# Weight columns in float32, an earlier cast of one batch, and eight output stores issued by ScalarE, in an attention and ReGLU kernel

## The chip, the cores and the metric

One core of one Trainium2 chip. The time is the device time of one execution in microseconds (us), and the median of several executions is quoted. All executions of the comparison before against after were in the fast state; slow ones elsewhere are named and left out.

## The reference

Causal attention for 8 batches of 8 heads (576 queries, 64 wide) over 16 "beacon" keys and values, which every query sees, and the batch's own 576; then a gated feed-forward layer over all 4608 rows (512 to 1536 to 512). Inputs and output are float32.

```python
k_all = np.concatenate([beacon_k, k], axis=2); v_all = np.concatenate([beacon_v, v], axis=2)
scores = scale * np.matmul(q, k_all.transpose(0, 1, 3, 2))
scores = np.where(causal, -1e9, scores)            # beacons never masked
a = np.exp(scores - scores.max(-1, keepdims=True)); a /= a.sum(-1, keepdims=True) + 1e-09
x = np.matmul(a, v_all)                            # then heads side by side: (4608, 512)
out = (np.maximum(x @ w_gate, 0.0) * (x @ w_val)) @ w_out
```

## The kernel before

It is one long, hand-ordered program. A list of steps says in which step a batch's attention and which groups of the feed-forward layer (FFN) run; the two are woven together so that TensorE always has matmuls. Loads, casts and transposes of a later batch are hung on these steps:

```python
def fetch(b, s0, late=1, held=False):
    at(s0, lambda: batches.update({b: Batch(b)}))
    for j, u in enumerate(LOADS):                  # k0 q1 k1 q2 k2 q3 k3 q0 k4 q4, then v0..v4
        s = s0 + j // 3
        at(s, lambda u=u, h=held and j == 0: batches[b].load(*u, h))      # SyncE
        at(s + late, lambda u=u: batches[b].cast(*u, pool))               # GpSimd
        if u[0] != "v":
            at(s + late + 1, lambda u=u: batches[b].turn(*u))             # SyncE, DMA transpose
fetch(2, s2 + 1, 3, True)
for b in range(3, B):
    fetch(b, BASE[b] - (7 if b == 3 else 5), 2 if b == 3 else 1)
```

GpSimd also runs the causal masks (`affine_select`) on what ScalarE's exponentials wrote. The end of the FFN, with its store:

```python
ob = pools["osb"].tile([P, d_model], FP32, name="ob")
nc.scalar.copy(ob[:, n], o[:, n])
m = self.m0 + ms * P
later_sp.append(                                   # issued at the next step
    lambda m=m, n=n, ob=ob: nc.sync.dma_start(out[m:m + P, n], ob[:, n]))
```

Every DMA signals a semaphore. SyncE and ScalarE take theirs in turn from one set of eight, GpSimd from another set; in the built program each DMA waits for the previous DMA on its own semaphore before it is issued (in the trace of before, SyncE's DMAs are on 101 and 103 to 109, GpSimd's on 111 to 118). A DMA raises its semaphore 16 times; it has landed when the last of the 16 has come.

## Time and profile before

| | before |
|---|---|
| time, median of 3 (range) | 391.03 us (390.40 to 392.42) |
| TensorE busy, of the profiled 391.3 us | 373.4 us (95%) |
| ScalarE busy | 190.6 us (49%) |
| waits of TensorE priced in the prediction | 4.10 us (stall B, 92 us), 1.7 us (stall A, 24 us) |

In a timeline each line gives start, duration, engine, source line, operation, output and inputs, how many of the same kind in a row, and in brackets how long the engine had been idle and what ended that. In the list of waits the three numbers are the total, the count and the longest. The change adds lines, so a source line of before has another number after: 391 becomes 403 (scores), 399 becomes 411 (exponential), 407 becomes 419 (mask), 454 becomes 466 (times v), 505, 508 and 514 become 517, 520 and 526 (FFN up, with its relu), 524, 527 and 530 become 536, 539 and 541 (FFN down, its copy, its store). Experiments built on one kernel have that kernel's numbers.

### The profile page before, as it was taken

Reading aid. Unit: us, or ns where it says so; the run is one execution under the profiler, and the core shown is the slowest. Engines: PE = TensorE matmul, PEld = TensorE weight load, DVE = VectorE, ACT = ScalarE, POOL = GpSimd, SP = SyncE. Lnnn points to the kernel's source line nnn. Section 1 sums busy time; section 2 is a strip of 40 time slices with the busy share of each in tenths; the row PEclk is TensorE's granted clock in tenths of the full one; section 3 lists DMA queues with packets and bytes.
Section 4 is the critical chain, followed back from the end, with each engine's and each line's share of the span. In section 5 each row is a group of like instructions: output and inputs, shape, how many; then the busy total and the mean of one; then the engine's idle time right before and its main releaser. Section 6 shows DMA issues by size and latency. Waiting matters only on the chain.

```text
span 391.3 us, 10203 instructions
## 1 busy us (share of the span) xinstructions
PE 373.4 (95%) x4297; PEld 189.9 (49%) x4297; DVE 199.2 (51%) x309; ACT 190.6 (49%) x271; POOL 123.0 (31%) x218
## 2 busy tenths in 40 slices
PE   7889999995999999999999999999999999999995
PEld 3454445542455555555555555555545544444443
DVE  4767577441374566346733674257525665412320
ACT  4763484336456553565447534655455523323321
POOL 1695464514443432252324242324320200000000
PEclk9989999998799999999999999999999999999999
DMA  7999999988896977697568855895310011002002
GB/s 214 194 206 186 171 186 218 167 190 185 157 170 138 207 141 164 139 217 131 108 156 179 158 110 126 193 138 128 86 55 2 2 55 54 2 28 80 3 27 87
DMA packets 148132, 50.44 MB, mean 129 GB/s; under 512 B 133616, under 2 KB 143600, under 8 KB 148080
## 3 DMA queue, kind: packets, MB, share of 16 engines
q1 hardware_dynamic: 139024, 44.48, 53.6%
q0 software_dynamic: 9056, 5.24, 9.8%
q8 instruction: 35, 0.57, 0.6%
q14 instruction: 17, 0.14, 0.2%
HBM read 38.34 MB, written 9.44 MB: 122 GB/s over the span
## 4 chain that ended last, share of the span: by engine, by line
PE 83%; DMA 7%; DVE 4%; SPq 2%; issue 1%; ACT 1%; POOL 1%; DVEq 0%
PE p L524 21%; PE p L505 20%; PE p L514 19%; PE p L454 8%; DMA wo<-in_moe_w_out_dram 4%; PE f L505 3%; PE p L391 3%; PE f L524 2%; DVE hT L516 2%; PE s L514 2%; DMA wide<-in_k_dram 1%; PE s L391 1%; PE ab L454 1%; DVE r L467 1%; SPq L275 1%
## 5 line engine op out<-in xcount | busy, mean ns | idle before, releaser
L516 DVE TENSOR_TENSOR hT<-g,p 128x512 bf16<-128x512 f32 x89 | 60.8, 684 | 107.2 <-PE p L514 76.5
L407 POOL TENSOR_SCALAR_AFFINE_SELECT e<-e 128x512 bf16<-128x512 bf16 (+2 forms) x80 | 46.3, 599 | 151.7 <-ACT e L399 151.5
L505 PE MATMUL p<-xT,wg 128*128 128x512 bf16 x356 | 93.2, 385 | 0.1
L514 PE MATMUL p<-xT,wv 128*128 128x512 bf16 x356 | 92.2, 382 | 0.0
L508 ACT ACTIVATE g<-p 128x512 f32<-128x512 f32 x89 | 52.8, 602 | 74.9 <-PE p L505 74.9
L524 PE MATMUL p<-wo,hT 128*128 128x512 bf16 (+1 forms) x396 | 85.5, 373 | 0.0
L399 ACT ACTIVATE e<-p 128x1024 bf16<-128x1024 f32 (+2 forms) x84 | 75.2, 966 | 14.8 <-PE p L391 14.8
L514 PEld LDWEIGHTS <-wv 128*128 128x128 bf16 x432 | 42.5, 99 | 53.4 <-issue 3.9
L467 DVE RECIPROCAL r<-p 128x256 f32<-128x256 f32 (+1 forms) x24 | 47.0, 1958 | 37.1 <-PE p L454 37.1
L524 PEld LDWEIGHTS <-hT 128*128 128x128 bf16 x444 | 42.1, 98 | 48.3 <-issue 0.8
L505 PEld LDWEIGHTS <-wg 128*128 128x128 bf16 x432 | 40.8, 99 | 49.3 <-issue 3.7
L527 ACT COPY ob<-p 128x512 f32<-128x512 f32 (+1 forms) x33 | 18.9, 573 | 66.3 <-PE p L524 66.3
L270 POOL CAST half<-raw 128x512 bf16<-128x512 f32 (+2 forms) x60 | 35.6, 619 | 14.5 <-DMA raw<-in_k_dram 9.7
L454 PEld LDWEIGHTS <-v 128*32 128x32 bf16 (+1 forms) x1408 | 27.8, 97 | 10.5 <-issue 5.3
L391 PEld LDWEIGHTS <-kT 64*128 64x128 bf16 x704 | 20.7, 97 | 25.1 <-issue 22.5
L454 PE MATMUL p<-e,v 128*32 128x80 bf16 (+4 forms) x1056 | 29.4, 231 | 1.6 <-DVE hT L516 1.0
L265 POOL CAST v<-raw 128x512 bf16<-128x512 f32 (+1 forms) x38 | 23.6, 644 | 13.3 <-DMA raw<-in_v_dram 13.3
L399 ACT ACTIVATE e<-s 128x1024 bf16<-128x1024 f32 (+2 forms) x28 | 25.6, 967 | 4.3 <-PE s L391 4.1
L391 PE MATMUL p<-qT,kT 64*128 64x80 bf16 (+3 forms) x528 | 23.0, 229 | 4.5 <-DMA qT<-half 4.1
L454 PE MATMUL p<-e,ones 128*32 128x80 bf16 (+4 forms) x528 | 24.3, 230 | 0.0
L505 PE MATMUL f<-xT,wg 128*128 128x512 bf16 x76 | 20.4, 393 | 0.3 <-DVE hT L516 0.3
L508 ACT ACTIVATE g<-f 128x512 f32<-128x512 f32 x19 | 11.4, 601 | 18.4 <-PE f L505 17.3
(81 smaller groups left out, 235.8 us busy)
## 6 DMA issues: line engine op xcount, KB each, us to landing
out_dram<-ob SPq DMA_DIRECT2D x35, 256.0 KB, 2.4
raw<-in_q_dram SPq DMA_DIRECT2D x25, 256.0 KB, 4.4
raw<-in_v_dram SPq DMA_DIRECT2D x24, 256.0 KB, 4.1
raw<-in_k_dram SPq DMA_DIRECT2D x19, 256.0 KB, 4.5
raw<-in_v_dram SPq DMA_DIRECT2D x8, 224.0 KB, 3.6
wo<-in_moe_w_out_dram POOLq DMA_DIRECT2D x2, 768.0 KB, 11.7
raw<-in_k_dram SPq DMA_DIRECT2D x6, 224.0 KB, 3.4
raw<-in_v_dram SPq DMA_DIRECT2D x8, 160.0 KB, 4.3
```

The costliest lines, as they stand in the source:

```text
L265: copy(self.v[:n, t].rearrange("p (h a d) -> p h a d", a=2, d=C), raw[:n].rearrange("p (h d a) -> p h a d", a=2, d=C))
L270: copy(h[:n], raw[:n])
L391: nc.tensor.matmul(self.s[:, a, c + j * n:c + (j + 1) * n], kT[rows, 2 * g + j, k0:k0 + P], qT[rows, 2 * g + j, q0:q0 + n], start=True, st ...
L399: nc.scalar.activation(e[:, :k * 4 * n].rearrange("p (k a x) -> p a k x", k=k, a=2), self.s[:, :, :k * 2 * n].rearrange("p a (k x) -> p a ...
L407: nc.gpsimd.affine_select(out=cols[:, :, :m], in_=cols[:, :, :m], pattern=[[0, 4], [1, m]], compare_op=ALU.is_ge, fill=0.0, base=base, cha ...
L454: nc.tensor.matmul(o[:, q0 - cq0:q0 - cq0 + n], w, e[:kr, 2 * (hh % 2) + hh // 2], start=(x == 0 and i == 0 and part != 1), stop=stop, ski ...
L467: nc.vector.reciprocal(self.r[:, :self.n], self.os[:, :self.n])
L505: nc.tensor.matmul(g[:, :n], wg[:, ki, nf * P:(nf + 1) * P], x[:, ki], start=(ki == 0), stop=(ki == KM - 1))
L508: nc.scalar.activation(gs[:, :n], g[:, :n], AF.Relu)
L514: nc.tensor.matmul(u[:, :n], wv[:, ki, nf * P:(nf + 1) * P], x[:, ki], start=(ki == 0), stop=(ki == KM - 1))
L516: nc.vector.tensor_mul(self.h[:, nf, c0:c1], gs[:, :n], u[:, :n])
L524: nc.tensor.matmul(o[:, n], self.h[:, nf, ms * P:(ms + 1) * P], wo[:, nf, n], start=(nf == 0), stop=(nf == NF - 1))
```

## The change

The intent is to relieve SyncE, whose one line of loads, transposes and stores is late for batch 2, and to let the weights' casting loads start behind the first loads. It has three parts: **W**, weights; **C**, the earlier cast of batch 2; **S**, the stores.

```diff
 # W: columns 256..384 of both matrices in float32 by SyncE, cast later; casting loads moved back
+        more_g, more_v = (load_w_more(x, 256, 384) for x in (moe_w_gate, moe_w_val))
-        after(3, lambda: load_w(wg, moe_w_gate, 256, 768))
-        after(3, lambda: load_w(wv, moe_w_val, 256, 768, (0,)))
-        after(4, lambda: first.cast("v", 4, pool))
-        mid[5] = lambda: load_w(wv, moe_w_val, 256, 768, (1,))
-        mid[6] = lambda: cast_w(wg, raw_g, 256, 1, pool)
+        after(3, lambda: first.cast("v", 4, pool))
+        after(3, lambda: load_w(wg, moe_w_gate, 384, 768))
+        after(4, lambda: load_w(wv, moe_w_val, 384, 768, (0,)))
+        mid[5] = lambda: load_w(wv, moe_w_val, 384, 768, (1,))
+        mid[6] = lambda: [cast_w(wg, raw_g, 256, 1, pool),
+                          cast_more(wg, more_g, 256, 384, pool)]
+        after(6, lambda: cast_more(wv, more_v, 256, 384, act))
 # C: batch 2's casts a step sooner, and a step's casts and loads all behind its FFN groups
-        fetch(2, s2 + 1, 3, True)
+        fetch(2, s2 + 1, 2, True)
-            for act_ in acts[:len(acts) // 2]:
+            early = len(acts) // 2 if s > BASE[2] else 0
+            for act_ in acts[:early]:
                 act_()
-            acts = acts[len(acts) // 2:]
+            acts = acts[early:]
 # S: the first two tiles' eight stores, issued by ScalarE right behind its copy
-                later_sp.append(
-                    lambda m=m, n=n, ob=ob: nc.sync.dma_start(out[m:m + P, n], ob[:, n]))
+                store = lambda e, m=m, n=n, ob=ob: e.dma_start(out[m:m + P, n], ob[:, n])
+                if self.m0 < 2 * M_TILE:
+                    store(nc.scalar)
+                else:
+                    later_sp.append(lambda store=store: store(nc.sync))
 # cut: load_w_more and cast_more themselves
```

More of the change, by code (lines that the diff above doesn't have):

```diff
@@ L363, in load_w_raw, with load_w_more, cast_more @@
         return raws
+    def load_w_more(src, n0, n1):
+        raw = stage.tile([P, d_model], FP32, name="raw")
+        for g in range(2):
+            nc.sync.dma_start(raw[:, 256 * g:256 * (g + 1)].rearrange("p (a n) -> p a n", a=2),
+                              src[2 * g * P:2 * (g + 1) * P, n0:n1].rearrange(
+                                  "(p a) n -> p a n", a=2))
+        return raw
+    def cast_more(dst, raw, n0, n1, cast):
+        cast(dst[:, :, n0:n1], raw.rearrange("p (k n) -> p k n", k=KM))
     def cast_w(dst, raws, n, g, cast):
```

## The prediction

> **What bounds the kernel now.** I read the page first: busy shares, then the slices.
>
> ```profile
> PE 373.4 (95%) x4297; PEld 189.9 (49%) x4297; DVE 199.2 (51%) x309; ACT 190.6 (49%) x271; POOL 123.0 (31%) x218
> PEclk9989999998799999999999999999999999999999
> ```
>
> TensorE is busy 95% of 391.3 us, nothing else above 51%: the end is set by TensorE's stream of matmuls, and only what leaves TensorE idle, or slow, can be won. It is idle for 391.3 - 373.4 = 17.9 us in all, and the granted clock dips twice, in slice 3 (19.6 to 29.3 us) and in slices 10 and 11 (88 to 108 us). Next, the list of waits for the whole run gives the idle places by cause (columns: us in total, times, longest):
>
> ```profile
> PE p L391 <- DMA qT<-half: 4.1, 1, 4.1
> PE ab L454 <- issue: 1.7, 1, 1.7
> PE f L524 <- DMA wo<-in_moe_w_out_dram: 0.5, 1, 0.5
> ```
>
> The rest is the start and shreds below 0.45 us. The first, **stall B**, is in TensorE's timeline (start, us, group; four matmuls of 512 columns are one group):
>
> ```profile
> 91.78 0.60 PE L391 MATMUL p<-qT,kT 64*128 64x128 bf16 x12
> 96.48 0.58 PE L391 MATMUL p<-qT,kT 64*128 64x80 bf16 x12 [4.10 <-DMA qT<-half]
> 97.00 1.89 PE L505 MATMUL p<-xT,wg 128*128 128x512 bf16 x4
> 98.68 1.91 PE L514 MATMUL p<-xT,wv 128*128 128x512 bf16 x4
> 100.39 1.81 PE L505 MATMUL p<-xT,wg 128*128 128x512 bf16 x4
> 102.04 1.03 PE L514 MATMUL p<-xT,wv 128*128 128x512 bf16 x4
> ```
>
> TensorE waits 4.10 us for the last transposed piece of batch 2's queries, then runs three groups at half speed (1.8 to 1.9 us against 1.03). The windows view prices that second part:
>
> ```profile
> 96.00:100.00 4.00, 3.52 (x20) 1.50 (x21) 0.00 (x0) 1.57 (x2) 3.15 (x7) 0.50 1.16 231
> 100.00:104.00 4.00, 3.84 (x30) 1.64 (x32) 1.38 (x2) 1.24 (x3) 0.87 (x2) 0.75 0.86 169
> ```
>
> PEclk is the seventh figure: 3.52 us at 0.50 and 4.00 us at 0.75 lose 3.52 x 0.50 + 4.00 x 0.25 = 2.76 us. Stall B costs 4.10 + 2.76 = **6.9 us**.
>
> Why the piece is late is in SyncE's timeline:
>
> ```profile
> 72.45 0.37 SPq L530 DMA_DIRECT2D out_dram<-ob  x1
> 72.86 1.36 SPq L275 DMA_TRANSPOSE kT<-half  x1
> ...
> 88.22 1.20 SPq L275 DMA_TRANSPOSE kT<-half  x1
> 89.47 0.57 SPq L250 DMA_DIRECT2D raw<-in_beacon_k_dram  x1
> ...
> 91.84 1.08 SPq L530 DMA_DIRECT2D out_dram<-ob  x1
> 93.02 1.20 SPq L275 DMA_TRANSPOSE qT<-half  x1
> ```
>
> SyncE issues without a pause from 52.8 to 97 us; ten transposes at 1.2 us each, v loads, four output stores and four loads of batch 3 stand in one line, and the last transpose is issued at 93.02 and lands 3.4 us later.
>
> **Stall A** is the 1.7 us at 24.0 us. "Issue" means no semaphore: TensorE stops in the middle of a group of eight equal matmuls. Some 255 TensorE instructions earlier, at 20.8 us, it had passed a like point, and a 16 KB packet of the instruction queue ran at 22.98 us, among full data queues. I read it as an instruction fetch that came late. It too is followed by a slow clock (mean 0.86 and 0.71 in 24 to 28 and 28 to 32 us), some 3.4 us at half, 1.7 us lost. A costs about 3.4 us.
>
> **What the Trainium skill says.**
> - "TensorE: Matmul & The Clock Gate", Part 1: the array's clock is either full or half, decided by a free-running window of 3.4 us; an idle window halves it. The trace agrees: the half clock after B lasts from 95.1 to 102.0, two such windows. So a stall[...] can cost 1.7 us on top.
> - "Runtime: NRT & Kernel Launch", Instruction fetch mechanics: instructions come in blocks of 256 (16 KiB) by DMA, and the fetch is normally hidden. The packet of 16 KB and the 255 instructions agree; in stall A it isn't hidden.
> - "DMA: Bandwidth & Descriptors", Issuing engines are not separate DMA queues: issuing from another engine saves only the issuing engine's time. Here that is worth something, since SyncE is the full one.
>
> **The change part by part.**
>
> *Stores by ScalarE.* The eight stores of the first two tiles leave SyncE; four of them stood in the critical line: 0.37 + 0.47 + 0.53 + 1.08 = 2.45 us less ahead of the last transpose. ScalarE, 49% busy, gets eight issues at about 0.5 us, 4 us in all. Each DMA also waits for the one eight issues before it on its semaphore (the built program shows these waits), so a store can hold ScalarE until an earlier load has landed; in 64 to 76 us that may delay an exponential by a microsecond or two, mostly beside other work.
>
> *Batch 2 cast a step sooner.* In the built order, the last transpose of batch 2 now stands ahead of batch 3's loads, which takes another 0.57 + 0.42 + 0.56 + 0.58 = 2.13 us out of its way, and the first three transposes come right after the tenth load, at about 69.7 instead of 72.9 us. I add up the line from there with the durations of before: 10 transposes x 1.25 + q load 0.6 + five v loads 3.9 gives 86.7 us. The last transpose is then issued at about 85.5 and lands by 89, 3 us before TensorE wants it. **Stall B goes: -6.9 us.**
>
> *The price of it.* GpSimd executes in order. In the built order of before, three casts precede the mask of step 16; now six do. The casts wait for loads:
>
> ```profile
> 65.18 0.62 POOL L270 CAST half<-raw 128x512 bf16<-128x512 f32 x1 [0.74 <-DMA raw<-in_k_dram]
> 65.75 0.48 POOL L407 TENSOR_SCALAR_AFFINE_SELECT e<-e 128x320 bf16<-128x320 bf16 x1
> ...
> 69.94 0.62 POOL L270 CAST half<-raw 128x512 bf16<-128x512 f32 x1 [2.31 <-DMA raw<-in_q_dram]
> 70.50 0.66 POOL L407 TENSOR_SCALAR_AFFINE_SELECT e<-e 128x320 bf16<-128x320 bf16 x1
> ```
>
> The sixth cast can't start before 69.94, when its load has landed, and that landing is set by transfers that the change leaves alone. So the mask moves from 65.75 to about 70.5 and ends at 71.0. TensorE wants it here:
>
> ```profile
> 68.97 0.25 PE L454 MATMUL ab<-e,v 80*32 80x80 bf16 x8
> ```
>
> That makes a **new stall of 71.05 - 68.97 = 2.1 us**, and at 6 in 10 a half-clock window, 0.6 x 1.7 = 1.0 us: **+3.1 us**. The second mask (after three more casts, 71.0 + 3 x 0.62 = 72.9) is wanted at 72.3 + 2.1 = 74.4, so no second stall.
>
> *Weights.* 128 columns of each matrix come in float32 by SyncE (512 KB, two casts of about 0.6 us on GpSimd and ScalarE, both beside other work at 25 to 27 us), and the casting loads carry a quarter less. HBM bytes are the same. The casting loads start one cast, 0.65 us, later. TensorE shows no gap at these weights before, so nothing is won there directly. What it may do is let the instruction fetch through: I give stall A 3 in 10 to shrink by most of its 3.4 us, of which the later waits for w_out (0.5 us now, its transfer fills the queues from 46 to 61 us) keep a third: 0.3 x 2.3 = -0.7. Against it, the v loads of batch 1 and then w_out end about 0.5 us later: +0.5.
>
> **Sum:** -6.9 + 3.1 - 0.7 + 0.5 = -4.0 us, 391.0 - 4.0 = **387.0 us**, 1.0% faster.
>
> **The rivals.**
> 1. *Stall B goes and nothing comes in its place.* For it: the sixth load may land sooner once SyncE's order has moved, and loads wander by a microsecond or two. Against: 2.31 us of waiting on that load in the trace, with GpSimd in order. Time: 391.0 - 6.9 = 384.1, and 382 or less if stall A also shrinks.
> 2. *The new wait takes it all.* The masks fall behind casts at both steps, ScalarE is held by its stores at the same time, and the clock halves for two windows: 2.1 + 1.0 more + 3.4 = 6.5 us, so 390.6. For it: 68 to 72 us is a stretch of short matmuls, where stall A's 1.7 us was enough to halve the clock. Against: from 72.5 us on there are 15 us of dense matmuls that need no mask.
> 3. *Stall A grows.* The extra 512 KB stand in SyncE's queue just when the fetch is asked for (20.8 us). A microsecond more would bring 388 to 389.
>
> **Range and chances.** Faster by over 2% means under 383.2: it needs stall B gone, no new stall and some of stall A, 0.12. Slower by over 2% would need 7.8 us of new waits, 0.02. The range from rival 1 with a little of stall A to rival 2 less a little is 383.2 to 389.8.
>
> **What would show it right or wrong.** Right: no wait of TensorE on qT<-half near 92 us and a clock of 1.00 from 92 to 104; the last qT transpose issued by 88; a wait of TensorE of 1.5 to 2.5 us at L466 (the former L454) near 69 us for an L419 mask that comes after the sixth cast; ScalarE still under 52%. Wrong: no gap at 69 us, which means that the sixth cast is not late and the gain is nearer 7 us; a gap near 24 us below 1 us, which means that the weight loads did bear on the fetch; or a TensorE wait on a store held by ScalarE, which I have counted as hidden.

## The result, and the profile after

The changed kernel took **395.06 us** (median of 4, 394.93 to 395.34), the kernel before 391.01 us (4 runs, 390.40 to 392.42): a ratio of 1.0099, 95% interval 1.0072 to 1.0127. Ratios here are the mean time of one kernel's fast runs over that of the other's of the same rounds, so not quite the ratio of the medians. A gain of 1.0% was predicted and a loss of 1.0% came, 5 us above the upper end of the range.

The page of the changed kernel, busy shares and slices:

```profile
PE 371.9 (94%) x4297; PEld 190.1 (48%) x4297; DVE 198.3 (50%) x309; ACT 191.0 (49%) x272; POOL 123.3 (31%) x219
PEclk9999999999998999999999999999999999999999
```

The clock dips of before are gone from slices 3, 10 and 11, and there is one new in slice 13. ScalarE is as little busy as before: its share does not show what went wrong. The list of waits does (the same view as of before; no wait of TensorE on qT<-half of batch 2 is left in it):

```profile
ACT e L411 <- DMA raw<-in_v_dram: 7.0, 1, 7.0
PE p L403 <- ACT e L411: 4.4, 2, 4.2
ACT g L520 <- DMA raw<-in_v_dram: 3.9, 1, 3.9
ACT e L411 <- DMA raw<-in_k_dram: 2.9, 1, 2.9
PE f L517 <- ACT g L520: 1.7, 1, 1.7
```

An exponential reads scores; it has no use for a raw v tile. Yet ScalarE waited 7.0 us for one to land ahead of an exponential, and TensorE 4.2 us for ScalarE. ScalarE's timeline shows what stands between:

```profile
107.62 0.59 ACT L539 COPY ob<-p 128x512 f32<-128x512 f32 x1 [2.05 <-PE p L536]
114.79 0.34 ACTq L541 DMA_DIRECT2D out_dram<-ob  x1
115.23 1.56 ACT L411 ACTIVATE e<-p 128x960 bf16<-128x960 f32 x2 [7.03 <-DMA raw<-in_v_dram]
```

The copy into `ob` ended at 108.21, but the store of `ob` was issued only at 114.79, and the exponential stood behind it. The trace names the store's semaphore, 107. The DMA before it on 107 was a v load of **batch 3**, which SyncE issued at 111.17 and which landed at 114.72, 0.07 us before the store was issued. The chain that ended last runs through just this (start, us, what):

```profile
111.17 3.55 DMA raw<-in_v_dram
114.72 0.02 issue
114.74 0.02 ACTq L541
114.75 0.04 issue
114.79 0.34 ACTq L541
...
115.23 0.84 ACT e L411
116.08 2.44 DMA kT<-half
118.52 0.02 issue
118.54 0.02 ACTq L541
118.56 0.04 issue
118.59 0.37 ACTq L541
118.96 0.05 issue
119.01 1.03 ACT e L411
```

Its second half shows the next store, issued at 118.59, 0.07 us after a transpose on its semaphore, 104, had landed. TensorE has the bill in its timeline:

```profile
80.62 1.02 PE L517 MATMUL f<-xT,wg 128*128 128x512 bf16 x4 [1.69 <-ACT g L520]
...
116.26 0.40 PE L403 MATMUL p<-qT,kT 64*128 64x256 bf16 x4 [4.15 <-ACT e L411]
```

The 1.69 us are the same thing earlier: a store issued at 79.53 waited for a v load of batch 2 on its semaphore (landed at 79.45), with a relu behind it. The 2.9 us on in_k_dram are one more hold, of a store issued at 69.78 behind a k load that landed at 69.71; TensorE waited only 0.15 us behind that one. The half clock after the second stall lasts from 116.8 to 120.2 us, one window.

What the prediction had said of batch 2 came true, with other sizes. SyncE's last transpose of batch 2 was issued here, ahead of batch 3's loads:

```profile
87.38 1.20 SPq L275 DMA_TRANSPOSE qT<-half  x1
88.64 0.58 SPq L250 DMA_DIRECT2D raw<-in_beacon_k_dram  x1
```

And GpSimd's sixth cast, with the mask behind it, and TensorE's wait for that mask:

```profile
67.55 0.61 POOL L270 CAST half<-raw 128x512 bf16<-128x512 f32 x1 [1.00 <-DMA raw<-in_q_dram]
68.12 0.47 POOL L419 TENSOR_SCALAR_AFFINE_SELECT e<-e 128x320 bf16<-128x320 bf16 x1
```

```profile
68.64 0.26 PE L466 MATMUL ab<-e,v 80*32 80x80 bf16 x8 [0.94 <-POOL e L419]
```

### The profile page after: what moved, and what is told of

It is laid out like the page before. It is cut to its first block, busy times and chain, and to the rows that moved or that the text cites. A ratio compares the mean times of both kernels' runs of the same rounds, so it can differ in the third digit from the quotient of the medians.

```text
span 393.6 us, 10209 instructions
## 1 busy us (share of the span) xinstructions
PE 371.9 (94%) x4297; PEld 190.1 (48%) x4297; DVE 198.3 (50%) x309; ACT 191.0 (49%) x272; POOL 123.3 (31%) x219
## 4 chain that ended last, share of the span: by engine, by line
PE 70%; DMA 16%; SPq 3%; POOL 3%; DVE 2%; ACT 2%; issue 2%; ACTq 0%; DVEq 0%; POOLq 0%
PE p L536 20%; PE p L517 19%; PE p L526 19%; PE p L466 6%; DMA raw<-in_v_dram 4%; DMA wv<-in_moe_w_val_dram 4%; DMA raw<-in_q_dram 3%; DMA raw<-in_k_dram 2%; PE p L403 2%; ACT e L411 2%; DVE hT L528 2%; SPq L250 1%; DMA wide<-in_k_dram 1%; SPq L275 1%; DMA hwide<-in_k_dram 1%
## 5 line engine op out<-in xcount | busy, mean ns | idle before, releaser
L517 PE MATMUL p<-xT,wg 128*128 128x512 bf16 x356 | 91.5, 379 | 0.2
L536 PE MATMUL p<-wo,hT 128*128 128x512 bf16 (+1 forms) x396 | 85.5, 373 | 0.2 <-ACT e L411 0.2
L466 PEld LDWEIGHTS <-v 128*32 128x32 bf16 (+1 forms) x1408 | 28.6, 99 | 11.0 <-issue 5.3
L466 PE MATMUL p<-e,v 128*32 128x80 bf16 (+4 forms) x1056 | 30.2, 235 | 1.5 <-DVE hT L528 1.0
L466 PEld LDWEIGHTS <-ones 128*32 128x32 bf16 (+1 forms) x704 | 19.7, 100 | 0.1
```

The source lines that it names most:

```text
L466: nc.tensor.matmul(o[:, q0 - cq0:q0 - cq0 + n], w, e[:kr, 2 * (hh % 2) + hh // 2], start=(x == 0 and i == 0 and part != 1), stop=stop, ski ...
L517: nc.tensor.matmul(g[:, :n], wg[:, ki, nf * P:(nf + 1) * P], x[:, ki], start=(ki == 0), stop=(ki == KM - 1))
L536: nc.tensor.matmul(o[:, n], self.h[:, nf, ms * P:(ms + 1) * P], wo[:, nf, n], start=(nf == 0), stop=(nf == NF - 1))
```

## The experiments

**Theory 1:** S alone loses the time. ScalarE's store waits for a semaphore whose DMA stands in SyncE's late line, so ScalarE, otherwise half idle, moves at SyncE's pace. **Theory 2:** W and C lose it (masks behind casts, weights later), and ScalarE's waits are a sign only. Every kernel was correct, and the kernel before ran beside each on the same chip.

### The changed kernel without S

```diff
-                if self.m0 < 2 * M_TILE: store(nc.scalar)   # all eight back to SyncE's later_sp
```

> The change without its third part: all output stores issued by SyncE again, weights and casts as changed. Theory 1 (a store on ScalarE waits for the completion of the DMA that used its semaphore before, a v load or a transpose that stands far back in SyncE's line, and holds ScalarE's exponentials and activations meanwhile): the waits of ScalarE on loads (7.0 and 3.9 us in the changed kernel), TensorE's stalls of 4.15 us at 112 us and 1.7 us at 79 us, and the half clock after 117 us go; that is about 8.5 us, so 386 to 388. SyncE gets four stores back ahead of batch 2's last transpose, so up to 1 us of wait near 92 us may come back. Theory 2 (the loss is from the weights or the casts, by more DMA traffic or a longer GpSimd line): no gain, 394 to 396.

Measured: 391.76 us, ratio 1.0050 (1.0010 to 1.0089). No wait of ScalarE on a raw tile is left at 78 or 115 us, so these came with S. But theory 1 expected 386 to 388, and that was missed; theory 2's 394 to 396 was missed too. The interval lies above 1: with SyncE's stores, W and C together are slower than the kernel before by 0.5%, half of what the whole change lost. The profile can't explain that, since it is of the fastest of the four runs (390.19). In it, TensorE waits mainly at two other places, the second in its timeline:

```profile
112.68 0.83 PE L403 MATMUL p<-qT,kT 64*128 64x256 bf16 x12 [1.84 <-DMA qT<-half]
```

This is for batch **3's** queries, a wait that the kernel before did not have in its first profile, and of 1.0 us in its second (in the first TensorE came to these matmuls at 116.89, the piece having landed at 114.10). The other is 1.13 us for weights at 51 us.

### The kernel before with S alone

```diff
+                if self.m0 < 2 * M_TILE: store(nc.scalar)
```

> The kernel before with the third part alone: the eight first stores issued by ScalarE. Theory 1: TensorE's 4.1 us wait for qT near 92 us shrinks, since SyncE's line is 2.5 us shorter, but ScalarE stands in ob stores for DMAs of SyncE's line, and a stall of 2 to 5 us with a half clock appears between 105 and 125 us: 389 to 394. Theory 2: the stores are harmless, the wait near 92 us shrinks, and the time falls to 387 to 389.

Measured: 396.77 us, ratio 1.0147 (1.0108 to 1.0186), above what theory 1 expected, and far from theory 2. By its mean S alone loses more than the whole change, though the intervals of 1.0147 and 1.0099 overlap. A line of TensorE's timeline, and one of the list of waits:

```profile
85.36 1.87 PE L505 MATMUL f<-xT,wg 128*128 128x512 bf16 x4 [4.60 <-ACT g L508]
```

```profile
ACT g L508 <- DMA raw<-in_v_dram: 5.9, 1, 5.9
```

With batch 2 still a step late, two stores wait for v loads of batch 2, from 72 to 84 us, in part where the prediction had looked, and the hold is 4.60 us on TensorE instead of "a microsecond or two, mostly beside other work". Two later stores wait for a v load and a transpose of batch 3 (issued at 118.07 and 122.21, when these had landed at 118.00 and 122.13); TensorE waits 1.84 us behind the second. The profile is of the slowest of the four runs (398.41).

### The changed kernel with the stores on GpSimd, and with half of them on ScalarE

```diff
-                    store(nc.scalar)
+                    store(nc.gpsimd)           # first kernel
-                if self.m0 < 2 * M_TILE:
+                if self.m0 < M_TILE:           # second kernel: four stores, the first tile's
```

> The changed kernel with the eight stores issued by GpSimd in place of ScalarE: same moment in the program, same bytes, but these DMAs have semaphores of their own, whose last users landed long ago. Theory 1: no wait of ScalarE on loads, none of TensorE on an exponential at 112 us: 385 to 388 (GpSimd pays about 0.7 us for each issue, ahead of masks). If early stores as such (their traffic among the loads) or any store off SyncE hurt: 392 to 396, with the stall still there.

> The changed kernel with only the first tile's four stores on ScalarE, the second tile's four back on SyncE. Theory 1: the stall at 112 us and the half clock after it go (about 6.5 us), the 1.7 us at 79 us stays: 388 to 389.5. Theory 2: 394 to 396.

Measured: 389.55 us, ratio 0.9975 (0.9945 to 1.0004), and 389.93 us, ratio 0.9981 (0.9950 to 1.0012). GpSimd's stores, on semaphores whose last users had landed by 60.9 us, wait for no earlier DMA; the second kernel keeps the hold at 78 us (1.99 us on TensorE) and loses the one at 115. Taking four stores from ScalarE is worth 5.1 us (395.06 to 389.93). The stall that went with them is 4.15 us; of the rest no line tells (each of the two profiles has one half-clock window, 3.4 x 0.5 = 1.7 us, at another place). Theory 1 holds for the stalls. But both missed their ranges (385 to 388, and 388 to 389.5): in the first kernel TensorE waits for batch 3's queries,

```profile
112.25 0.83 PE L403 MATMUL p<-qT,kT 64*128 64x256 bf16 x12 [2.05 <-DMA qT<-half]
```

### W and C one at a time, and the kernel before once more

> The kernel before with only the earlier cast of batch 2. If stall B (4.1 us and its half clock) is really worth 6.9 us and only the stores by ScalarE spoil the change: 384 to 387 us, no wait on qT of batch 2, a wait of 1 to 2 us for a mask near 69 us. If TensorE, coming sooner to batch 3, has to wait there for batch 3's transposes, as the run with SyncE's stores showed (1.8 us and a half clock at 111 to 120 us): 388 to 391 us, with a wait of 1.5 to 3 us on qT<-half between 105 and 122 us.

> The kernel before with only the weight part (first 384 columns in float32, casting loads later). If the weight part is near nothing: 390 to 392 us, with stall B's wait on qT<-half near 92 us still there and stall A (1 to 2 us at 24 us, no semaphore) as often as not. If it is the weight part that ate the gain of the run with SyncE's stores: 393 us or more, with waits on wv or xT between 37 and 53 us that the kernel before hasn't.

> The kernel before, unchanged, to see how far two sets of runs of one kernel differ and whether its stalls A and B are in every profile. If both are fixed: a wait on qT<-half of 3 to 5 us near 92 us, a stop of 1 to 2 us without a semaphore near 24 us, ratio within 0.3% of 1. If stall A or the clock windows wander: stall B there, stall A absent or elsewhere, span up to 3 us off the first profile's 391.3.

Measured: C alone 389.12 us, ratio 0.9962 (0.9923 to 1.0002), with a wait of 2.5 us on batch 3's queries; W alone 391.65 us, ratio 1.0051 (0.9990 to 1.0113), one of its four runs at 395.26; the kernel before against itself 390.13 us, ratio 0.9977 (0.9938 to 1.0015). So a ratio may be off by 0.2% by chance, and neither part is told from nothing here. (The half clock at 111 to 120 us that the first expectation names was in the run with GpSimd's stores, from 113.3 to 116.7, not in that with SyncE's.) The second profile of before has a span of 388.7 us where the first had 391.3. Its stall B, in TensorE's timeline:

```profile
95.01 0.39 PE L391 MATMUL p<-qT,kT 64*128 64x80 bf16 x12 [3.26 <-DMA qT<-half]
95.34 1.04 PE L505 MATMUL p<-xT,wg 128*128 128x512 bf16 x4
96.21 1.03 PE L514 MATMUL p<-xT,wv 128*128 128x512 bf16 x4
```

It is 3.26 us, and **no half clock follows**: the groups of four run in 1.03 us at once. Stall A is there too, with 1.5 us and no half clock behind it. The first profile had been of an execution of 393.04 us, 2 us above the median; its clock losses are not in every run. In the profile of W alone, stall B is 3.33 us and one half-clock window follows: two windows, none and one in three profiles.

W shows in two waits. In the seven profiles of kernels with W, TensorE's wait with no semaphore near 24 us averages 0.5 us, in the eight without W 1.0 us; the wait for w_val near 50 us averages 1.0 us with W and 0.3 us without. The line for the kernel with W alone, from the list of waits:

```profile
PE f L526 <- DMA wv<-in_moe_w_val_dram: 1.3, 2, 1.0
```

What W wins at one place it seems to give back at the other; this is a hint only, since the second wait goes from none to 1.9 us between single profiles.

### C a second time, and v of batch 3 by GpSimd

```diff
+                eng = nc.gpsimd if x == "v" and b == 3 else nc.sync     # on top of C alone
+                eng.dma_start(raw[p0:p1].rearrange("p (h d) -> p h d", d=D),
```

> The kernel before with the earlier cast of batch 2 alone, a second time, on the chip of the other run. If its gain is real: ratio 0.994 to 0.998 with an interval below 1, a wait on qT<-half of 1.5 to 3 us at batch 3. If the first run's 0.9962 was chance: ratio within 0.998 to 1.002.

> The kernel before with the earlier cast of batch 2, and batch 3's six v loads issued by GpSimd (its semaphores aren't SyncE's), some 4 us of issuing out of SyncE's line. If SyncE's line is the bound at batch 3: the transpose of q tile 3 comes about 3 us sooner, v lands no later, no wait over 0.7 us on qT<-half or on a mask between 105 and 122 us, and 1.5 to 3 us less than with the earlier cast alone, so 386 to 388 us. If the transfers themselves are the bound (the transposes and loads share the data queues): a wait of 1.5 to 3 us stays, on qT<-half or on L408's masks, and the time is 389 to 391 us.

Measured: C again 389.88 us, ratio 0.9993 (0.9952 to 1.0033): it is not told from no gain. VectorE runs the same sequence of 309 instructions in both kernels, so the same place can be compared. Against the second profile of before, C's second one is 3.8 us ahead at 99 us, behind where stall B was, and 0.1 to 0.7 us ahead at 125 us (in C's first profile, without a half clock at batch 3, 1.9 of 3.6 us are left there). Between, TensorE waited for batch 3 and had a half clock from 113.3 to 116.7:

```profile
112.10 0.83 PE L391 MATMUL p<-qT,kT 64*128 64x256 bf16 x12 [2.98 <-DMA qT<-half]
```

The transpose that it waited for landed at 112.01, against 113.74 in the second profile of before: only 1.7 us sooner, while TensorE came to it 3.7 us sooner. C had changed the **order** of SyncE's line, not its length. It had put batch 2's last transpose ahead of batch 3's loads.

With the six v loads out of that line it was no better: 392.78 us, ratio 1.0056 (1.0019 to 1.0093), and a longer wait at the same place. Here is that wait, and then the windows view from 100 to 112 us, C alone first, then this kernel (DMA share and GB/s are the last two figures):

```profile
115.02 0.83 PE L392 MATMUL p<-qT,kT 64*128 64x256 bf16 x12 [3.48 <-DMA qT<-half]
```

```profile
100.00:112.00 12.00, 8.86 (x186) 5.10 (x188) 6.73 (x8) 5.09 (x7) 5.78 (x10) 1.00 0.82 139
```

```profile
100.00:112.00 12.00, 9.85 (x192) 5.31 (x192) 7.79 (x9) 5.47 (x8) 11.83 (x19) 1.00 1.17 208
```

The transpose of q tile 3 was issued sooner, at 108.66 instead of 109.58, but landed 6.2 us after its issue instead of 2.4, beside v loads that GpSimd had issued from 105.3 us on and that landed from 110.6 to 114.0. The first sentence of the expectation failed. The second (the transfers are the bound) fits the wait, though the time came out above it; GpSimd, now busy 11.83 of these 12 us (the sixth figure), is a rival for part of the loss that was not tested.

### Batch 3 sooner, and its v later

```diff
-            fetch(b, BASE[b] - (7 if b == 3 else 5), 2 if b == 3 else 1)
+            fetch(b, BASE[b] - (7 if b == 3 else 5), 1)                 # first kernel (stores on GpSimd, W and C)
-                at(s, lambda u=u, h=held and j == 0: batches[b].load(*u, h))
+                at(s + (b == 3 and u[0] == "v"),                        # the other three
+                   lambda u=u, h=held and j == 0: batches[b].load(*u, h))
```

> The changed kernel with the eight stores issued by GpSimd, and batch 3's casts and transposes a step sooner too (SyncE's line there was what TensorE waited for, 2.05 us, then a half clock of 3.4 us). If SyncE's line is what gave the gain back at batch 3: no wait on qT<-half between 105 and 122 us and 2 to 4 us less than with the stores on GpSimd alone, so 386 to 388 us. If SyncE can't keep up whatever the order: the wait moves (to a mask behind the casts, or to batch 4's transposes) and the time stays at 389 to 391 us.

> The earlier cast of batch 2 alone, the eight stores by GpSimd, and batch 3's v loads a step later, so that the transpose of q tile 3, for which TensorE waits at batch 3, has two v loads and the beacon's fewer (about 2.8 us of SyncE's line) ahead of it. If SyncE's line is what gives the gain back: no wait over 0.7 us on qT<-half between 105 and 122 us and 386 to 388.5 us. If the wait only changes its cause (v cast late, a mask behind it): 389 to 391 us with a wait on L407's masks or on v between 110 and 125 us.

> The same without moving the stores (all by SyncE, as in the kernel before): the earlier cast of batch 2 and batch 3's v loads a step later. If the stores' place matters little once they are not on ScalarE: within 0.3% of the kernel with GpSimd's stores, 386.5 to 389 us. If the four stores in SyncE's line (2.45 us) matter: 1 to 2 us more than it, with a wait on qT<-half between 105 and 122 us of 1 us or more.

> The changed kernel, stores by ScalarE, with batch 3's v loads a step later. In the built program the store near 115 us then has, eight issues before it on its semaphore, not a v load of batch 3 but the transpose of its k tile 3. If ScalarE is held by that semaphore: the exponential behind it waits for kT<-half and no longer for raw<-in_v_dram, for a like time (3 to 8 us), TensorE waits for it, and the time stays at 392 to 396 us. If ScalarE was held by the v loads' load on memory, or by the store's own transfer: the hold at 108 to 115 us goes or halves, and the time is 389 to 391 us.

Measured: batch 3 sooner 395.70 us, ratio 1.0098 (1.0048 to 1.0148; one slow run of 400.82 left out). The wait on qT is gone, and GpSimd's casts, waiting for q and v loads in their order, hold the mask. GpSimd first, then TensorE:

```profile
110.03 0.60 POOL L270 CAST half<-raw 64x512 bf16<-64x512 f32 x1 [3.76 <-DMA raw<-in_q_dram]
112.02 0.63 POOL L265 CAST v<-raw 128x512 bf16<-128x512 f32 x1 [1.38 <-DMA raw<-in_v_dram]
113.34 0.63 POOL L265 CAST v<-raw 128x512 bf16<-128x512 f32 x1 [0.69 <-DMA raw<-in_v_dram]
113.92 1.76 POOL L419 TENSOR_SCALAR_AFFINE_SELECT e<-e 128x512 bf16<-128x512 bf16 x3
```

```profile
114.61 0.41 PE L466 MATMUL p<-e,v 128*32 128x128 bf16 x8 [4.58 <-POOL e L419]
```

This is the stall that the prediction had placed at 69 us, at another place and twice as long.

With v later, C and GpSimd's stores: 390.89 us, ratio 1.0007 (0.9971 to 1.0043); with v later and C alone: 390.57 us, ratio 1.0006 (0.9968 to 1.0045). Without W, then, no difference shows whether SyncE or GpSimd issued the stores; both times lie above the ranges hoped for. The wait only changed its cause, here to a mask behind v's casts (the list of waits of the second of them):

```profile
PE p L454 <- POOL e L407: 2.7, 1, 2.7
PE p L391 <- DMA qT<-half: 1.8, 1, 1.8
```

The last of the four, the changed kernel with v later, tests theory 1 at its root. ScalarE's instructions come in the same order as in the changed kernel; batch 3's v loads come later, and so the DMA ahead of the store on semaphore 107 is another one, the transpose of k tile 3. Measured: 398.25 us, ratio 1.0198 (1.0155 to 1.0241). The store was issued at 113.58:

```profile
106.16 0.59 ACT L539 COPY ob<-p 128x512 f32<-128x512 f32 x1 [2.05 <-PE p L536]
113.58 0.34 ACTq L541 DMA_DIRECT2D out_dram<-ob  x1
114.02 1.56 ACT L411 ACTIVATE e<-p 128x960 bf16<-128x960 f32 x2 [7.28 <-POOL v L265]
```

That transpose landed at 113.51, 0.07 us before. The v load on which the store had waited in the changed kernel was not even issued until 113.91, so it was not that load as such. The profile's name for the releaser, a cast of v, is not the one expected: it names the last event that it saw before the exponential, and the store's own wait has no line. The next store, on semaphore 104, was issued at 119.75, after the v load on 104 had landed at 119.67. TensorE waits 4.41 and 2.49 us. The hold has about the same length with another DMA on the semaphore, as theory 1 said. The semaphore events of all the traces agree: in none of the 15 is a DMA seen to be issued before the one ahead of it on its semaphore had landed, and in the four kernels with stores by ScalarE, at least 16 of the 28 stores were issued less than 0.08 us after that landing. The time came out 2 us above its range; the second store, held likewise, now cost TensorE another 2.49 us, with a second half-clock window behind it (122.0 to 125.4).

## Why the prediction was wrong

- **The step that failed** is the cost of the stores by ScalarE: "a store can hold ScalarE until an earlier load has landed; in 64 to 76 us that may delay an exponential by a microsecond or two, mostly beside other work". The term was 0. It measured 1.69 + 4.15 us of TensorE's time and one half-clock window (1.7 us), 7.5 us in the profile; taking the stores to GpSimd gave 5.5 us back (395.06 to 389.55), taking them to SyncE 3.3 (to 391.76), and S alone on the kernel before cost 1.47%, 5.7 us. The mechanism had been seen and named; what was not asked is **which** DMA is on that semaphore. The answer stood in the order of issue: one of SyncE's, eight issues back, and SyncE's line was the very one that the prediction called late. In the stretch that was looked at, the price was fair: one store was held there for 2.5 us, and TensorE waited 0.15 us behind it. The holds that cost were the one to 79.5 us, just behind that stretch, and the one from 108 to 115 us, which was not looked for at all. A "TensorE wait on a store held by ScalarE" stands among the prediction's own signs of being wrong.
- **Stall B goes, -6.9 us.** It went, and the transpose came in time, though 1.9 us later than worked out (issued at 87.38 instead of 85.5). The size was wrong twice. The 2.76 us of half clock are not in every execution; the second profile of before had 3.26 us of idle time and no half clock. And the sum had no term for what comes next: once S is out of the account, the two runs of C alone (ratios 0.9962 and 0.9993) show that most of it was given back at batch 3, where the transfers came only 1.7 us sooner.
- **The new mask stall, +3.1 us.** The mechanism was right and the size too large: 0.94 us, no half clock. The sixth cast began at 67.55, not 69.94. The landing of its load had been taken as fixed from one profile: 69.88 in the first of before, but 67.13 in the second profile of that same kernel, and 67.50 in the changed one. So the smaller stall is in part luck (the waits for this mask among the kernels with C went from none to 1.7 us).
- **Weights, -0.2 us.** Near nothing, as said, though the place was w_val, not w_out. The gap near 24 us, 0.2 us in the changed kernel, is below the 1 us named as a sign that the weight loads bear on it. The interval of W alone (-0.1% to +1.1%) can't say more.
- **The sum.** Without the stores' term, and with C worth about 1 us instead of 3.8, the same working would have given 391.0 - 0.9 - 0.2 = 389.9. That is where the two kernels with GpSimd's or half of the stores came out (389.55, 389.93), but the one with SyncE's stores took 391.76, and its 1.9 us more are not explained. The stores by ScalarE add 5.1 to 5.5 against the first two and 3.3 against the last. So most of the loss is shown to be S, and up to 1.9 us of it stays open. The rival "the new wait takes it all" had the hold of ScalarE in it, but at 390.6 and with the masks of 68 to 72 us.

Of the versions tried, the best (C alone, and the stores on GpSimd or half of them on ScalarE) lie 0.1 to 0.4% under the kernel before with intervals that reach 1, so none is shown to beat it. What stays open is whether anything short of fewer bytes or fewer transposes between 52 and 120 us would; four attempts to reorder them or to issue them elsewhere only moved the wait or made it longer.

## What to carry to other kernels

In a program built like this one, a DMA that an engine issues makes that engine wait for whatever is ahead of it on the DMA's semaphore; before giving a store to a half-idle engine, find that other DMA in the built order and ask when it will land, and prefer an issuer whose semaphores are its own. When a stall is removed, look for the next thing that the bound engine will want from the same late line, and check that it too comes sooner. Price a stall's half clock from more than one execution.

## What the Trainium skill lacked or had wrong

- "DMA: Bandwidth & Descriptors", Issuing engines are not separate DMA queues, says that issuing from several engines saves only the issuing time. Here it cost: ScalarE stood 7.0 us at one store, and eight stores by ScalarE lost 1.47% on the kernel before. The page speaks of DMAs that share a semaphore only as a danger to the data; it has no word on what it costs in time when two issuing engines take their semaphores from one set.
- The same page, section Anatomy of one DMA, says that any wait for a semaphore happens on the issuing sequencer, before dispatch. The trace agrees: with batch 3's v later, the store was issued 0.07 us after its semaphore's transpose landed, and the exponential behind it began 0.4 us later. What the section lacks is that the compute instructions of that engine stand behind the wait.
- "TensorE: Matmul & The Clock Gate", Part 1, has the half-clock window right (3.4 us) and says that it is free-running. That one stall may or may not bring a half clock isn't there: a stall of 3.26 us with no half clock behind it and one of 4.10 us with two windows were the same stall in two executions.
- No page gives a duration for a DMA transpose that runs beside loads: the transpose of q tile 3 landed 2.4 us after its issue where the DMA share from 100 to 112 us was 0.82, and 6.2 us after it where that was 1.17.
